# The last batch's Fourier folds queued on VectorE behind the third low part of the first MLP chunk

## The chip, the cores and the metric

The kernel runs on one core of a Trainium2 chip. The metric is the device time of one execution in microseconds (us). The core has a matrix engine, TensorE (PE in the profile), three engines for elementwise work, VectorE (DVE), ScalarE (ACT) and GpSimd (POOL), and SyncE (SP), whose queue issues nearly all DMA transfers here. Each engine works through its own queue in order and waits on semaphores for the others. Operands lie in SBUF, and TensorE's results land in PSUM.

## The reference, cut to what matters

Three blocks follow each other: windowed attention, a block that mixes by a Fourier transform and an MLP, and a gated MLP. The change lies in the second one, and in its overlap with the end of the first:

```python
def _moe_ref(x, w_ch1, w_ch2):              # x: (4, 576, 512)
    X = np.fft.fft(x, axis=1)
    X = np.fft.fft(X, axis=2)
    u = x + np.real(X)
    mu = np.mean(u, axis=-1, keepdims=True)
    var = np.mean((u - mu) ** 2, axis=-1, keepdims=True)
    un = (u - mu) / np.sqrt(var + 1e-06)
    ch = np.maximum(un @ w_ch1, 0.0) @ w_ch2
    return u + ch
```

The weights come as 64-bit floats, and the products are made in three passes with operands split in a high and a low part, so that they are nearly those of float32.

## The kernel before

The residual stream lies in SBUF as `uT`, channels on partitions, 4 batches of 576 tokens side by side. The MLP runs over six chunks of 384 tokens. A chunk begins as soon as its tokens are normalized, so the Fourier transforms of the later batches, the layer norms of the later chunks and the decoding of later weights run beside the MLP of the first chunks. Five kinds of work meet in the stretch that the change touches, from about 136 to 170 us.

**The MLP** (`mlp`, line 683). For each block f of 128 hidden channels, 12 matmuls (`mm3`, lines 130 to 132) make `h` in one of two PSUM buffers; ScalarE takes the relu into the high part `rh` (L717), and VectorE makes the low part `rl` from `h` and `rh` (L718). Three blocks later, at most, 12 matmuls add the second layer into four banks `acc`, and after the last block of a phase VectorE adds them to `uT` (L703). The third `h` needs the first one's buffer back, and so the first `rl`.

**The Fourier transform** (`dft`, line 501). The input is first folded in E, O and F. For the last batch the fold is made in one go, inside the first step of `dft(3)`, by five VectorE instructions: E and O (L464, L465), the sums with the reversed half (L469, L470), and a copy of one column (L473), with two small ones on GpSimd (L471, L474). Then `fold_split` makes high parts on ScalarE (`eh` L482, `oh` L484, `grow` L488) and low parts on GpSimd (`el` L483, `ol` L485, `grow` L489). TensorE reads them later as `g<-tab,eh` and so on; L536 to L538 are the copies and splits between the transform's two stages.

**The layer norm** (`ln`, line 624 on) transposes a chunk into PSUM (L637), copies it to SBUF (L639 on ScalarE), normalizes (L650), transposes it back (L656), copies (L659) and splits it in `xhm` (L661, ScalarE) and `xlm` (L662, GpSimd).

**The decode** (`raw` and `halves`, lines 157 to 172) turns 64-bit weights into a high and a low part, 256 columns at a time: a load `dec_s` on SP's queue (L162), `dec_g` on ScalarE (L165), two VectorE steps (L166, L167), the high part on ScalarE (L171) and the low part on VectorE (L172). It has four staging buffers and four `dec_w`.

**The banks** `g`. The transposes and the transform's matmuls share two PSUM buffers (`gps`, `bufs=2`), given out in turn.

The order within each engine's queue isn't written out. The kernel gives priorities (`soon` raises the layer norms, the transforms and the decode of `rest`, and a relu has one of its own), and a scheduler with a model of durations lays the instructions out when the program is built. `tc.issue_after(i)` adds one constraint to that: what is traced inside it, on i's engine, is placed behind i.

Of the kernel before, what the change touches and what calls it, by code (L numbers as in the profile page):

```python
# [42 lines left out]
RATE = 1.0  # L43
NV = 0
VL = 2
LAG, XPT = (1, 2, 3), 0
PACE = 1.0
FP = ()
# [65 lines left out]
class Kernel:  # L114
# [188 lines left out]
    def load_attn(self, n):  # L303
        if n < B * NB:
# [5 lines left out]
            if j % 3 == 0:  # L310
                self.load_k(b, j // 3)
        if VL <= n < B * NB + VL:
            b, j = divmod(n - VL, NB)
            if j % 2 == 0:
# [352 lines left out]
    def open_mlp(self):  # L667
        self.bp, self.mlp_es = self.pool("mlp", side="right")
        self.low = self.nc.vector
        self.bps, self.bps_es = self.pool("mlp_ps", side="right", space=PSUM)  # L670
        self.rs_ = [(self.bp.tile([128, 384], F32R, name=f"rh{i}"), self.bp.tile([128, 384], F32R, name=f"rl{i}")) for i in range(3)]
        self.nr = self.nq = 0

    def rpair(self, n):
        self.nr += 1
        return self.rs_[self.nr % n]
# [6 lines left out]
    def mlp(self, before, last):  # L683
        nc = self.nc
        V, A = nc.vector, nc.scalar
        pend = []
        st = {}

        def second(g, n, f, rh, rl):
            t = self.sets[f % 8]  # L690
            start, size = CHUNKS[n]
            first, last = f == PHASES[g][0][0], f == PHASES[g][0][-1]
            if first:
                st["acc"] = [self.bps.tile([128, 512], F32, tag=f"acc{c}", name="acc") for c in range(4)]
            acc = st["acc"]
            for c in range(4):
                s = slice(128 * c, 128 * c + 128)
                self.mm3(acc[c][:, 0:size], [(t[:, 2, s], t[:, 3, s], rh, rl)], first=first, last=last)
            if last:
                with self.tc.high_priority(URGENT):  # L700
                    for c in range(4):
                        x = self.uT[:, c, start:start + size]
                        v = V.tensor_tensor(out=x, in0=acc[c][:, 0:size], in1=x, op=ALU.add)  # L703
                self.marks = [v.ins]

        for g, (fs, ns) in enumerate(PHASES):
            for n in ns:
                before(g, n)
                xh, xl, size = self.xh[n], self.xl[n], CHUNKS[n][1]
                for f in fs:  # L710
                    t = self.sets[f % 8]
                    ps = self.bps.tile([128, 512], F32, tag="h", bufs=2, name="h")
                    o = ps[:, 0:size]
                    self.mm3(o, [(t[:, 0, 128 * k:128 * k + 128], t[:, 1, 128 * k:128 * k + 128], xh[:, k], xl[:, k]) for k in range(4)])
                    rh, rl = self.rpair(3)
                    with self.tc.high_priority(URGENT):
                        a = A.activation(out=rh, in_=o, func=AF.Relu)  # L717
                        v = V.scalar_tensor_tensor(out=rl, in0=o, scalar=0.0, in1=rh, op0=ALU.max, op1=ALU.subtract)  # L718
                        self.marks = [a.ins, v.ins]
                    pend.append((g, n, f, rh, rl))  # L720
                    yield 5 * size
                    if len(pend) > 2:
                        second(*pend.pop(0))
                        yield 5 * size
        while pend:
            second(*pend.pop(0))
            if last is not None:
                last()
                last = None
            yield 1500  # L730
# [522 lines left out]
def emit(tc, aps):  # L1253
    with ExitStack() as ctx:
        k = Kernel(ctx, tc, aps)
# [44 lines left out]
        def soon(gen):  # L1300
            while True:
                with tc.high_priority(SOON):
                    w = next(gen, None)
                if w is None:
                    return
                yield w * RATE

        def weave(*gens):
            gens = list(gens)
            while gens:  # L1310
                for g in list(gens):
                    w = next(g, None)
                    if w is None:
                        gens.remove(g)
                    else:
                        yield w / 2

        def norms(*ns):
            for n in ns:
                yield from norm(n)  # L1320

        def norm(n):
            for u in UNITS_OF[n]:
                yield from soon(k.ln(u))
            done.add(n)

        def rest():
            yield from soon(k.decode_f(3))
            done.add(0)
            yield from weave(norms(1, 2), soon(k.dft(2)))  # L1330
            yield from soon(k.dft(3))
            k.dft_es.close()
            p, es = k.pool("late", side="left")
            ctx.enter_context(es)
            k.open_tail(p)
            for i in (6, 7, 8):
                k.open_set(i, p)
            for n in TAIL:
                yield from norm(n)
# [13 lines left out]
        def behind(gen):  # L1353
            marks = None
            while True:
                marks = marks or k.marks
                with ExitStack() as st:
                    for i in marks:
                        st.enter_context(tc.issue_after(i))
                    w = next(gen, None)  # L1360
                if w is None:
                    return
                yield w

        def u_forms(gap):
            yield from spaced(k.decode_u(0), gap)
            gen = k.decode_u(1)
            for _ in range(2):
                next(gen)
                yield gap  # L1370
            while not st7:
                yield None
            for _ in gen:
                yield gap
            for kc in range(2):
                yield from spaced(k.decode_in(kc), gap)
# [16 lines left out]
        def raws2():  # L1393
            for e in range(2):
                k.raws(2, e)
                yield 1000

        rest_ = rest()
        lanes = [[rest_], [decodes((4, 5), D45)], []]

# [7 lines left out]
        def before(g, n):  # L1408
            while n not in done:
                next(rest_)  # L1410
            if n == PHASES[g][1][0]:
                drain(lanes[1])
                if g == 1:
                    lanes[2].append(when(behind(blocks1()), lambda: 3 in done))
                elif g == 2:
                    lanes[1].append(behind(pair(6, G6)))
                    lanes[2].append(behind(blocks()))
                elif g == 3:
                    drain(lanes[0], lanes[2])
                    lanes[1].append(pair(8, G8))  # L1420
                    lanes[2].append(raws2())
# [114 lines left out]
```

## Time and profile before

| | us |
|---|---|
| median of 3 runs | 767.67 (766.78 to 767.84) |
| the profiled execution | 767.85 |
| its span | 766.1 |
| TensorE busy | 746.9 (97%) |
| VectorE busy | 526.7 (69%) |
| ScalarE busy | 352.3 (46%) |
| GpSimd busy | 192.5 (25%) |
| TensorE's granted clock, mean | 0.999 of full speed |

The profile is of one execution. The span runs from its first to its last instruction, and 1.75 us lie around it. The table's busy times overlap. An engine's timeline has one row for an instruction or for a run of equal ones: when it starts, how long it takes, and in brackets how long the engine had been idle and what ended that. An instruction's time in it includes what it waits for after its start.

### The profile page before, as it was taken

To read this page: it belongs to the slowest core of one execution; us is meant where nothing else is said; L and a number is where in the kernel's file an instruction comes from. 1 tells how busy PE (TensorE), PEld (TensorE's weight loads), DVE (VectorE), ACT (ScalarE), POOL (GpSimd) and SP (SyncE) were. 2 spreads that over 40 slices of the span, in tenths; PEclk is the share of its full clock that TensorE was granted. 3 is DMA by queue.
4 is the path that set the end of the run, shared out by engine and by line. 5 is a ranking of instruction groups with operands and counts; after the bars stand their busy time and mean duration, and the time that the engine had idled before them with its cause. 6 is when DMAs were issued, how large, how long until landed. Compare 5 with 4: busy or idle time off the path is not lost.

```text
span 766.1 us, 13950 instructions
## 1 busy us (share of the span) xinstructions
PE 746.9 (97%) x4994; PEld 719.3 (94%) x4994; DVE 526.7 (69%) x1482; ACT 352.3 (46%) x839; POOL 192.5 (25%) x246
## 2 busy tenths in 40 slices
PE   7899799899999999999999999999999999999998
PEld 6788698899999999999999999999999898999897
DVE  4768866983445599884688657646987679674662
ACT  5797986745235556341245324124646454231210
POOL 2354453534213450064421112021102111010100
PEclk9999999999999999999999999999999999999999
DMA  9997761443015888585837923753110141114023
GB/s 263 309 303 237 223 212 45 123 125 124 1 30 179 282 275 295 185 318 172 308 133 297 352 93 136 293 217 124 51 62 24 48 132 32 63 32 134 11 73 123
DMA packets 84773, 123.37 MB, mean 161 GB/s; under 512 B 24416, under 2 KB 61664, under 8 KB 84704
## 3 DMA queue, kind: packets, MB, share of 16 engines
q1 hardware_dynamic: 82912, 119.13, 46.6%
q0 software_dynamic: 576, 2.97, 1.1%
q8 instruction: 39, 0.64, 0.4%
q10 hardware_dynamic: 1216, 0.39, 0.2%
q14 instruction: 30, 0.25, 0.1%
HBM read 91.79 MB, written 30.67 MB: 160 GB/s over the span
## 4 chain that ended last, share of the span: by engine, by line
PE 89%; DVE 5%; DMA 2%; ACT 2%; issue 1%; SPq 0%; POOL 0%; ACTq 0%; DVEq 0%; POOLq 0%
PE w L130 7%; PE w L132 7%; PE w L131 7%; PE g L130 7%; PE g L132 6%; PE g L131 6%; PE c L132 6%; PE c L130 6%; PE c L131 6%; PE acc L132 3%; PE acc L131 3%; PE h L130 3%; PE h L131 3%; PE h L132 3%; PE acc L130 3%; PE sc L328 3%
## 5 line engine op out<-in xcount | busy, mean ns | idle before, releaser
L171 ACT ACTIVATE set<-dec_w 128x256 fp32r<-128x256 f32 x111 | 45.0, 414 | 68.6 <-PE w L131 31.0
L846 POOL TENSOR_TENSOR u<-u 128x384 f32<-128x384 f32 x15 | 18.6, 1243 | 185.0 <-ACT u L845 126.4
L619 POOL TENSOR_TENSOR rq<-rq,mhalf 128x1 f32<-128x1 f32 (+1 forms) x24 | 15.9, 664 | 150.1 <-DVE rq L618 149.0
L335 ACT ACTIVATE s<-s,mx 128x128 f32<-128x128 f32 x144 | 47.6, 392 | 8.3 <-DVE mx L333 8.1
L172 DVE TENSOR_TENSOR set<-dec_w,set 128x256 fp32r<-128x256 f32 x99 | 44.1, 453 | 9.8 <-ACT set L171 3.6
L165 ACT ACTIVATE dec_g<-dec_s 128x256 f32<-128x256 f32 x88 | 37.4, 428 | 26.5 <-DMA dec_s<-in_wi 10.8
L131 PE MATMUL acc<-rl,set 128*128 128x384 f32 x144 | 48.7, 338 | 0.0
L132 PE MATMUL acc<-rh,set 128*128 128x384 f32 x144 | 48.6, 337 | 0.0
L333 DVE CUSTOM_DVE_ANT_0 s<-sc,mask 128x128 f32<-128x128 f32 x144 | 33.2, 284 | 21.6 <-PE sc L328 14.1
L130 PE MATMUL acc<-rh,set 128*128 128x384 f32 x144 | 46.2, 337 | 0.0
L328 PE MATMUL sc<-k,q 128*128 128x128 f32 x288 | 40.5, 284 | 4.9 <-DVE mx L333 2.4
L167 DVE SCALAR_TENSOR_TENSOR dec_w<-dec_g,dec_w 128x256 int32<-128x256 int32 x88 | 42.0, 480 | 3.6 <-ACT dec_g L165 3.3
L846 DVE TENSOR_TENSOR u<-w,u 128x384 f32<-128x384 f32 x44 | 24.3, 552 | 27.1 <-POOL u L846 22.6
L328 PEld LDWEIGHTS sc<-k,q 128*128 128x128 f32 x288 | 36.1, 195 | 6.9 <-issue 3.1
L893 DVE TENSOR_TENSOR uT<-g,uT 128x384 f32<-128x384 f32 x36 | 19.3, 552 | 28.2 <-PE g L132 28.1
L718 DVE SCALAR_TENSOR_TENSOR rl<-h,rh 128x384 fp32r<-128x384 f32 x36 | 19.8, 550 | 23.8 <-ACT rh L717 23.7
L130 PE MATMUL c<-set,set 128*128 128x320 f32 (+2 forms) x120 | 36.2, 303 | 0.0
L132 PE MATMUL c<-set,set 128*128 128x320 f32 (+2 forms) x120 | 36.0, 303 | 0.0
L131 PE MATMUL c<-set,set 128*128 128x320 f32 (+2 forms) x117 | 35.1, 302 | 0.0
L166 DVE TENSOR_SCALAR dec_w<-dec_s 128x256 int32<-128x256 int32 x88 | 31.2, 362 | 4.5 <-DMA dec_s<-in_wo 2.9
L355 PEld LDWEIGHTS pv<-v,pts 128*64 128x64 f32 x576 | 23.5, 137 | 7.8 <-issue 4.2
L845 ACT ACTIVATE u<-w 128x384 f32<-128x384 f32 x29 | 14.1, 486 | 36.0 <-PE w L132 35.1
(383 smaller groups left out, 2604.4 us busy)
## 6 DMA issues: line engine op xcount, KB each, us to landing
dec_s<-in_w SPq DMA_DIRECT2D x64, 256.0 KB, 3.5
v<-in_v SPq DMA_DIRECT2D x16, 520.0 KB, 5.8
xht<-xb SPq DMA_DIRECT2D x10, 768.0 KB, 8.9
xhm<-xb SPq DMA_DIRECT2D x10, 768.0 KB, 7.2
xlm<-xb SPq DMA_DIRECT2D x8, 768.0 KB, 7.9
k<-in_k SPq DMA_DIRECT2D x11, 512.0 KB, 6.5
xf<-u SPq DMA_DIRECT2D x18, 256.0 KB, 2.9
p<-xf SPq DMA_DIRECT2D x24, 192.0 KB, 3.4
```

The lines of the kernel that those rows point to most:

```text
L130: mm(out, lhsT=lh, rhs=rh, start=first and i == 0, stop=False)
L131: mm(out, lhsT=lh, rhs=rl, start=False, stop=False)
L132: mm(out, lhsT=ll, rhs=rh, start=False, stop=last and i == n - 1)
L165: nc.scalar.activation(out=g, in_=s[:, :, 1].bitcast(F32), func=AF.Prelu, scale=2.0 ** -112, alpha=-2.0 ** 32)
L166: nc.vector.tensor_scalar(out=w, in0=s[:, :, 0], scalar1=29, scalar2=None, op0=ALU.logical_shift_right)
L167: nc.vector.scalar_tensor_tensor(out=w, in0=g[:].bitcast(I32), scalar=3, in1=w, op0=ALU.logical_shift_left, op1=ALU.bitwise_or)
L171: self.nc.scalar.activation(out=hi, in_=f, func=AF.Copy)
L172: self.low.tensor_tensor(out=lo, in0=f, in1=hi, op=ALU.subtract)
L328: nc.tensor.matmul(sc[:, hp], lhsT=q[:, hp].rearrange("p a b -> p (a b)"), rhs=k[:, hp, o:o + 128], start=True, stop=True)
L333: nc.vector.tensor_tensor_reduce(out=s[:, hp], in0=sc[:, hp], in1=mask, scale=-0.125, scalar=1e30, op0=ALU.add, op1=ALU.min, accum_out=mx[ ...
L335: nc.scalar.activation(out=s[:, hp], in_=s[:, hp], func=AF.Exp, bias=mx[:, hp:hp + 1], scale=-1.0)
L846: add = lambda eng, o, i, j: eng.tensor_tensor(out=o, in0=i, in1=j, op=ALU.add)
```

## The change

The MLP keeps a list of its low-part instructions. The first step of the last batch's transform, which holds its fold, is traced inside `issue_after` of the third of them (`BEHIND = 2`, counted from 0), so the fold's VectorE instructions must stand behind it. The rest of the transform is traced as before. No instruction is added or removed; the scheduler lays out the stretch around the fold anew, on all engines.

```diff
+BEHIND = 2
...
         self.nr = self.nq = 0
+        self.lows = []
...
                         v = V.scalar_tensor_tensor(out=rl, in0=o, scalar=0.0, in1=rh, op0=ALU.max, op1=ALU.subtract)
                         self.marks = [a.ins, v.ins]
+                    self.lows.append(v.ins)
...
-            yield from soon(k.dft(3))
+            yield from soon(held(k.dft(3)))
...
+        def held(gen):
+            with tc.issue_after(k.lows[BEHIND]):
+                w = next(gen)
+            yield w
+            yield from gen
```

Line numbers of the changed kernel are 1 higher than before from line 46 on, 2 from line 674 on and 3 from line 720 on, so L464 is L465 there, and L718 is L720.

On VectorE, from the fold to the first low part, the order before is this (`rl_2201` belongs to the first block's `h`; `set_...` are weights):

```order
L464 TENSOR_TENSOR E<-uT 128x1152
L465 TENSOR_TENSOR O<-uT 128x1152
L166 TENSOR_SCALAR dec_w<-dec_s 128x256 x2
L469 TENSOR_TENSOR E<-E 128x2x288
L166 TENSOR_SCALAR dec_w<-dec_s 128x256 x2
L470 TENSOR_TENSOR F<-O 128x2x288
L473 COPY F<-O 128x2
L167 SCALAR_TENSOR_TENSOR dec_w<-dec_g,dec_w 128x256 x2
L718 SCALAR_TENSOR_TENSOR rl_2201<-h,rh_2200 128x384
```

After the change VectorE has the fold between the third low part (`rl_2199`) and the fourth (again `rl_2201`, the first one's buffer):

```order
L720 SCALAR_TENSOR_TENSOR rl_2199<-h,rh_2198 128x384
L465 TENSOR_TENSOR E<-uT 128x1152
L466 TENSOR_TENSOR O<-uT 128x1152
L167 TENSOR_SCALAR dec_w<-dec_s 128x256
L173 TENSOR_TENSOR set_2190<-dec_w,set_2190 128x256
L168 SCALAR_TENSOR_TENSOR dec_w<-dec_g,dec_w 128x256
L173 TENSOR_TENSOR set_2190<-dec_w,set_2190 128x256
L470 TENSOR_TENSOR E<-E 128x2x288
L471 TENSOR_TENSOR F<-O 128x2x288
L474 COPY F<-O 128x2
L720 SCALAR_TENSOR_TENSOR rl_2201<-h,rh_2200 128x384
L168 SCALAR_TENSOR_TENSOR dec_w<-dec_g,dec_w 128x256
```

Ahead of the first low part there now stand four L166 and two L167 of the decode alone.

On ScalarE, at the end of the decode's run beside the first chunk, the order before has the layer norm's first copy of the next chunk, L639, ahead of the last two `set` copies:

```order
L171 ACTIVATE set_2191<-dec_w 128x256
L165 ACTIVATE dec_g<-dec_s 128x256
L537 ACTIVATE tail0b<-cp 33x256
L171 ACTIVATE set_2191<-dec_w 128x256
L165 ACTIVATE dec_g<-dec_s 128x256
L639 ACTIVATE u<-g 128x512
L171 ACTIVATE set_2191<-dec_w 128x256 x2
L717 ACTIVATE rh_2202<-h 128x384
```

After the change it stands behind them, and the split of the fold comes just before:

```order
L483 ACTIVATE eh<-E 128x2x289
L489 ACTIVATE grow<-gr 1x289
L662 ACTIVATE xhm<-u 128x4x128
L537 ACTIVATE cp<-g 33x256
L485 ACTIVATE oh<-F 128x2x289
L172 ACTIVATE set_2191<-dec_w 128x256
L166 ACTIVATE dec_g<-dec_s 128x256
L538 ACTIVATE tail0b<-cp 33x256
L172 ACTIVATE set_2191<-dec_w 128x256 x2
L640 ACTIVATE u<-g 128x512 x2
L719 ACTIVATE rh_2202<-h 128x384
```

Both copies of the layer norm now follow each other directly, behind every `set` copy.

## Rows read from the trace of the kernel before

**Rows 1.** The page, chain that ended last, its share by engine.

```profile
PE 89%; DVE 5%; DMA 2%; ACT 2%; issue 1%; SPq 0%; POOL 0%; ACTq 0%; DVEq 0%; POOLq 0%
```

**Rows 2.** TensorE's waits, 134 to 210 us: us in total, times, longest.

```profile
PE h L130 <- DVE rl L718: 1.5, 1, 1.5
...
PE g L656 <- DVE uT L568: 0.2, 1, 0.2
```

**Rows 3.** Timeline of TensorE: start, us, engine, line, operation, tiles, count, [idle before].

```profile
141.88 0.86 PE L130 MATMUL acc<-rh,set 128*128 128x384 f32 x4
...
145.35 0.44 PE L130 MATMUL h<-xh,set 128*128 128x384 f32 x1 [1.46 <-DVE rl L718]
...
149.62 0.33 PE L130 MATMUL h<-xh,set 128*128 128x384 f32 x1
149.79 0.34 PE L131 MATMUL h<-xl,set 128*128 128x384 f32 x1
...
160.10 0.60 PE L637 MATMUL g<-ident,uT 128*128 128x128 f32 x4
```

**Rows 4.** Timeline of VectorE, the fold and the first low part.

```profile
136.94 1.36 DVE L464 TENSOR_TENSOR E<-uT 128x1152 f32<-128x1152 f32 x1 [0.55 <-ACT uT L386]
138.22 1.35 DVE L465 TENSOR_TENSOR O<-uT 128x1152 f32<-128x1152 f32 x1
...
140.52 0.75 DVE L469 TENSOR_TENSOR E<-E 128x576 f32<-128x576 f32 x1
...
142.21 0.75 DVE L470 TENSOR_TENSOR F<-O 128x576 f32<-128x576 f32 x1
142.88 1.29 DVE L473 COPY F<-O 128x2 f32<-128x2 f32 x1
...
144.75 0.54 DVE L718 SCALAR_TENSOR_TENSOR rl<-h,rh 128x384 fp32r<-128x384 f32 x1
```

**Rows 5.** Timeline of VectorE, third and fourth low part, decode steps between.

```profile
152.09 0.54 DVE L718 SCALAR_TENSOR_TENSOR rl<-h,rh 128x384 fp32r<-128x384 f32 x1
152.55 0.41 DVE L172 TENSOR_TENSOR set<-dec_w,set 128x256 fp32r<-128x256 f32 x1
...
154.64 0.41 DVE L167 SCALAR_TENSOR_TENSOR dec_w<-dec_g,dec_w 128x256 int32<-128x256 int32 x1
154.97 0.28 DVE L166 TENSOR_SCALAR dec_w<-dec_s 128x256 int32<-128x256 int32 x1
155.78 0.91 DVE L172 TENSOR_TENSOR set<-dec_w,set 128x256 fp32r<-128x256 f32 x1 [0.53 <-ACT set L171]
156.61 1.54 DVE L167 SCALAR_TENSOR_TENSOR dec_w<-dec_g,dec_w 128x256 int32<-128x256 int32 x1
...
158.82 0.54 DVE L718 SCALAR_TENSOR_TENSOR rl<-h,rh 128x384 fp32r<-128x384 f32 x1
```

**Rows 6.** Timeline of GpSimd, low parts of fold, layer norm and transform.

```profile
141.19 0.95 POOL L489 TENSOR_TENSOR grow<-gr,grow 1x289 fp32r<-1x289 f32 x1 [0.56 <-ACT grow L488]
142.22 1.93 POOL L483 TENSOR_TENSOR el<-E,eh 128x578 fp32r<-128x578 f32 x1
...
154.68 1.73 POOL L662 TENSOR_TENSOR xlm<-u,xhm 128x512 fp32r<-128x512 f32 x1 [2.66 <-ACT xhm L661]
156.37 1.50 POOL L485 TENSOR_TENSOR ol<-F,oh 128x578 fp32r<-128x578 f32 x1
157.94 0.81 POOL L538 TENSOR_TENSOR tail0b<-cp,tail0b 33x256 fp32r<-33x256 f32 x1
```

**Rows 7.** Timeline of ScalarE, first decode steps and the layer norm's copy.

```profile
138.93 0.75 ACT L165 ACTIVATE dec_g<-dec_s 128x256 f32<-128x256 f32 x2
...
158.82 0.59 ACT L639 ACTIVATE u<-g 128x512 f32<-128x512 f32 x1
```

**Rows 8.** The staged weights `dec_s`, 125 to 175 us: time from issue to landing.

```profile
DMA to landing us min/median/max: 2.6/3.4/4.9
```

**Rows 9.** The tile `eh`, 170 to 215 us: count, ns min/median/max, first and last start.

```profile
L130 PE MATMUL g<-tab,eh x6: 279/288/386, 183.5 to 186.0; 128*128 128x258 f32 x4, 128*33 128x258 f32 x2
```

## The prediction

> **What bounds the kernel now.** I read the page's chain first: TensorE (PE) holds 89% of it [rows 1], so a saved or added microsecond counts where it ends or makes a wait of TensorE. The list of TensorE's waits in the stretch in which the change lies comes next: the longest is 1.5 us, a first-layer matmul that waits for the low part `rl` of a relu [rows 2]. The timeline shows the place: the third `h` group starts at 145.35 after 1.46 us of idleness [rows 3]. There are two `h` buffers in PSUM, so the third group needs the first group's low part, and that stands on VectorE (DVE) behind the folds. VectorE's timeline shows them: E and O at 136.94 and 138.22, the reversed pair at 140.52 and 142.21, a copy of two elements that takes 1.29 us, and only at 144.75 the low part [rows 4]. The reader should see there that the folds are not the whole delay: decode steps stand between them, and several VectorE instructions are longer than their shape asks for. GpSimd (POOL) explains those. The copy ends at 144.17, and POOL's `el` ends at 144.15 [rows 4, 6]; a decode step of 0.41 us takes 1.54 us from 156.61 to 158.15 while POOL's `ol` runs to 157.87 [rows 5, 6]. So the two engines take turns, and POOL's work is a term of any sum for VectorE.
>
> **What the change removes.** The folds' five VectorE instructions leave the place ahead of the first low part. Behind them now stand four first decode steps (L166) whose data lie in SBUF, two L167, and then `rl`. ScalarE (ACT) gives the two `dec_g` at 138.93 to 139.68 [rows 7] and the first relu right after, some half a microsecond, so the first low part comes at about 140.1 in place of 144.75, and TensorE, which has work until 143.89 (145.35 less 1.46), no longer waits. Removed: 1.46 us.
>
> **What it adds.** The folds now stand behind the third low part and ahead of the fourth, and the scheduler has moved decode, layer-norm copies and fold splits with them. Which wait ends last then? The candidate is the second group of transposes L637. It needs a `g` bank, which ScalarE's first copy L639 gives back. In the order before, that copy stood ahead of the last decode copies L171; now it stands behind all of them, and each L171 needs an L167 of VectorE. Before, L639 ran at 158.82 and the transposes at 160.10 without a wait [rows 3, 7]. I add up when L639 can run now.
>
> Steps by themselves: L167 or L172 take 0.34 us from start to start, L166 0.21 (0.28 less the overlap of 0.07), a low part 0.47 [rows 5]; E and O together 2.55, L469 and L470 0.67 each (0.75 less 0.08 of overlap), the copy some 0.1 without POOL [rows 4]. POOL by itself, its wait for VectorE taken off: `ol` 1.18 (from 156.69, where L172 ends, to 157.87); `el` 1.19 (L470 ends at 142.96, `el` at 144.15); `bl` or tail 0.60 (158.15 to 158.75); `grow` 0.67 (0.95 less 0.28); `xlm` 1.16 (from 155.25, where L166 ends, to 156.41) [rows 4 to 6]. I call them 1.2, 1.2, 0.6, 0.7 and 1.2. For `gr`, which works on one partition like `grow`, I take 0.7, and 0.2, an estimate, for its one-element copy.
>
> First, the start. VectorE has read the staged weights early, so the next load waits only for ScalarE's first `dec_g`, done at about 139.35, and for the queue: 139.4. Landing takes 2.6 to 4.9 us, median 3.4 [rows 8]; I take 3.0, since the queue is empty then: 142.4. From there to the third low part stand five L166 (1.05), eight L167 or L172 (2.7), two low parts (0.94) and POOL's `xlm` and `bl` (1.8): 6.5, so 148.9. Then E and O 2.55, four decode steps 1.2, POOL's `xlm`, `bl`, `gr` and its copy 2.7, the reversed pair and copy 1.45, the fourth low part 0.47: 8.4, so 157.3. Behind it eight decode steps (three L166, five L167 or L172) 2.3, against POOL's `el`, `grow`, `xlm`, `ol` and tail, 4.9: 164.5. ScalarE's last L171 (0.3) and L639 (0.59 [rows 7]) put the transposes at 165.4.
>
> What would cost nothing? In the new order 76 and not 69 matmuls of 384 columns stand between the four `acc` matmuls at 141.88 and these transposes, counted in the two orders; the seven take 0.17 each (149.62 to 149.79), 1.2 us [rows 3]. So the transposes may come at 160.10 + 1.2 = 161.3 with no net change, and at 159.85 for the whole gain of 1.46. The sum says 165.4: a loss of 4.1.
>
> How good is such a sum? I make the same one for the order before. From E at 136.94 to the first low part: own work 5.5 and POOL 2.8 give 145.2, and the trace has 144.75 [rows 4]. From the third low part, 152.09, to the fourth: 0.47, twelve decode steps 3.56 and POOL's three instructions 3.0 give 159.1, and the trace has 158.82 [rows 5]. The sums are 0.45 us too long in 7.8 and 0.3 in 6.7, about 5%. Over the 23 us from 142.4 that is 1.15: the transposes come at 164.25, a loss of 2.95. I take **+2.9 us**. It includes the 1.46 removed. It should last to the end, since TensorE is the chain and its order behind the hunk is unchanged.
>
> Other edits. The same number of instructions runs on each engine. The last batch's transform reads `eh` first at 183.5 [rows 9], and in the sum `eh` is ready near 157 and `ol` near 163: more than 20 us hide the folds' delay, and without that cover all of it, some 15 us, would show. The queue SP has the same loads in a slightly other order; a later landing is in the bounds below.
>
> **A rule beside the rows.** Two VectorE instructions at 154.64 and 154.97 take 0.41 and 0.28 us undisturbed though POOL's `xlm` had begun at 154.68 [rows 5, 6]: POOL does not get its turn after each instruction. The Trainium skill, page "SBUF — State Buffer", section "SBUF: two separate sides", calls the pair of ports that VectorE and GpSimd share an exclusive lock, held for a whole instruction by whichever starts first. By that rule strictly taken the turns alternate and the uncorrected sum, +4.1, holds; the row at 154.97 speaks for less.
>
> **The rivals.** *VectorE keeps its pace, and no new wait comes.* What costs is POOL's work between VectorE's steps, 1.8 + 2.7 + 4.9 = 9.4 us in the sum. If a third of it, 2.95, falls into VectorE's idle time (it waits for loads and for ScalarE) the transposes come by 161.3 and the change is level; with half, 4.4, by 159.85, and only the 1.46 gain stands: 767.85 - 1.46 = 766.4, by the median 766.2. For it speaks the row at 154.97; against it the 1.54 and 0.91 us steps right behind [rows 5]. Not slower: 26% for level, and 6% for more than that, where the small wait of 0.2 us behind a VectorE step of the transform [rows 2] goes as well: 1.66 us, 766.0.
>
> *The loads land late.* With the longest landing, 4.9 us [rows 8], the first step is 1.9 later, and all behind it: +4.8, 772.5. The crowded stretch speaks for it, the empty queue at 139.4 against it: 10%.
>
> **How the numbers follow.** The profiled execution took 767.85 us, its span 766.1 and 1.75 around it; 767.85 + 2.9 = 770.75. It lies 0.18 above the median of the runs, so I predict 770.6 us: 58%. Late loads add 10% on the same side, so slower by over 0.2% (1.5 us, about what a measurement can tell from no change) has 68%, within 0.2% 26%, faster 6%. The forecast's own range is 769.2 (half of the loss) to 771.8 (the sum uncorrected). The range of all cases runs from 766.6, near the whole gain, which leaves about a tenth below, to 772.4, just short of the latest loads.
>
> **What would show it.** Right: the first low part at about 140, no wait of the third `h` group; the fourth low part at 156 to 158; POOL busy almost without a break from there for 5 us, and decode steps of over 1 us beside it; the second L637 transposes near 164 with the longest wait of the stretch, put down to ScalarE's L639. Wrong: these transposes at or before 161, or a first `h` wait that remains. If an `h` or `acc` matmul waits for the fourth low part instead, the mechanism is the folds themselves and not the copy behind the decode.

## The result and the profile after

The changed kernel takes 771.1 us (median of 12 runs, 769.15 to 775.47) against 767.75 us (12 runs, 766.33 to 770.89) of the kernel before, run beside it: a ratio of 1.0051, 95% interval 1.0038 to 1.0064. It is slower, by 3.4 us by the medians' difference; 770.6 us had been forecast. The profiled execution took 770.25 us, its span 768.4 us, so 1.85 us lie around it.

Two profiled executions also differ where nothing was changed, so I compare all kernels here between two fixed points: the start of the four `acc` matmuls in one row, which was at 141.88 before [rows 3], and the start of the `tail0b` matmul of the second half of a later transform, at 197.89 before. That is 56.01 us before, and 59.07 after (141.66 to 200.73): **+3.06 us**. The granted clock is 1.00 between the two points in both. Ahead of the first point the changed kernel's execution was 0.22 us shorter and behind the second about half a microsecond, which leaves the 2.4 us between the two profiled times.

TensorE's waits after, 134 to 210 us (us in total, times, longest), which answer [rows 2]:

```profile
PE g L638 <- ACT u L640: 2.4, 1, 2.4
PE h L131 <- ACT xhm L662: 1.0, 1, 1.0
PE xt L385 <- DVE rq L621: 0.8, 1, 0.8
PE h L132 <- POOL xlm L663: 0.5, 1, 0.5
PE g L657 <- DVE uT L569: 0.2, 1, 0.2
```

The wait of the third `h` group for the low part is gone; `xt` and L657 wait as before. Three waits are new, and TensorE's timeline, in the columns of [rows 3], shows where:

```profile
156.29 0.34 PE L132 MATMUL acc<-rl,set 128*128 128x384 f32 x1
157.67 0.63 PE L131 MATMUL h<-xhm,set 128*128 128x384 f32 x2 [1.03 <-ACT xhm L662]
...
159.55 0.34 PE L133 MATMUL acc<-rh,set 128*128 128x384 f32 x1
160.38 0.45 PE L132 MATMUL h<-xlm,set 128*128 128x384 f32 x1 [0.50 <-POOL xlm L663]
...
161.37 0.34 PE L131 MATMUL h<-xhm,set 128*128 128x384 f32 x1
164.12 0.66 PE L638 MATMUL g<-ident,uT 128*128 128x128 f32 x4 [2.42 <-ACT u L640]
```

They sum to 3.95 us, less the 1.46 removed 2.49. Between the two fixed points TensorE's busy time rises as well, from 54.31 to 54.88 us with the same work, and 2.49 + 0.57 is the whole 3.06. Most of the 0.57 belongs to the waits too. A row's time is 0.33 to 0.34 us though the next matmul of this shape starts after 0.17 [rows 3], so the idle time in brackets begins some 0.17 us after TensorE has begun to stand still. From start to start, less the usual step, the three waits cost 1.21, 0.66 and 2.58 us. The one before cost 1.62, counted from this row of the trace before to the third `h` group at 145.35:

```profile
143.61 0.28 PE L132 MATMUL g<-tab,ol 128*128 128x256 f32 x1
```

The first rows behind a wait also take 0.06 to 0.11 us longer to the next one (0.28 for 0.17 at 160.38, 0.41 for 0.35 at 164.12). Counted in this way the new waits make 4.73 us and the old one 1.73, and the difference, 3.00, is all but 0.06 of the 3.06.

VectorE's timeline after, from the third low part on (it answers [rows 4, 5]):

```profile
148.18 0.54 DVE L720 SCALAR_TENSOR_TENSOR rl<-h,rh 128x384 fp32r<-128x384 f32 x1
148.64 1.34 DVE L465 TENSOR_TENSOR E<-uT 128x1152 f32<-128x1152 f32 x1
149.91 1.34 DVE L466 TENSOR_TENSOR O<-uT 128x1152 f32<-128x1152 f32 x1
151.18 0.28 DVE L167 TENSOR_SCALAR dec_w<-dec_s 128x256 int32<-128x256 int32 x1
...
153.06 0.75 DVE L471 TENSOR_TENSOR F<-O 128x576 f32<-128x576 f32 x1
153.72 1.26 DVE L474 COPY F<-O 128x2 f32<-128x2 f32 x1
154.90 0.54 DVE L720 SCALAR_TENSOR_TENSOR rl<-h,rh 128x384 fp32r<-128x384 f32 x1
155.37 0.48 DVE L168 SCALAR_TENSOR_TENSOR dec_w<-dec_g,dec_w 128x256 int32<-128x256 int32 x1
155.77 2.48 DVE L167 TENSOR_SCALAR dec_w<-dec_s 128x256 int32<-128x256 int32 x2
158.16 1.03 DVE L173 TENSOR_TENSOR set<-dec_w,set 128x256 fp32r<-128x256 f32 x1
159.12 1.49 DVE L168 SCALAR_TENSOR_TENSOR dec_w<-dec_g,dec_w 128x256 int32<-128x256 int32 x1
160.54 1.40 DVE L167 TENSOR_SCALAR dec_w<-dec_s 128x256 int32<-128x256 int32 x1
...
162.20 0.94 DVE L168 SCALAR_TENSOR_TENSOR dec_w<-dec_g,dec_w 128x256 int32<-128x256 int32 x1
```

Behind the fourth low part at 154.90 most of the decode steps that take 0.28 and 0.41 us elsewhere take 0.9 to 1.5 us. GpSimd's timeline shows its side (as [rows 6]):

```profile
150.14 4.82 POOL L663 TENSOR_TENSOR xlm<-u,xhm 128x512 fp32r<-128x512 f32 x1 [3.38 <-ACT xhm L662]
154.92 0.64 POOL L539 TENSOR_TENSOR bl<-cp,bh 128x256 fp32r<-128x256 f32 x1
155.53 0.97 POOL L472 TENSOR_TENSOR gr<-O 1x288 f32<-1x288 f32 x1
156.45 0.17 POOL L475 COPY gr<-O 1x1 f32<-1x1 f32 x1
156.58 1.31 POOL L484 TENSOR_TENSOR el<-E,eh 128x578 fp32r<-128x578 f32 x1
157.97 0.95 POOL L490 TENSOR_TENSOR grow<-gr,grow 1x289 fp32r<-1x289 f32 x1
158.99 1.34 POOL L663 TENSOR_TENSOR xlm<-u,xhm 128x512 fp32r<-128x512 f32 x1
160.29 1.50 POOL L486 TENSOR_TENSOR ol<-F,oh 128x578 fp32r<-128x578 f32 x1
161.87 0.98 POOL L539 TENSOR_TENSOR tail0b<-cp,tail0b 33x256 fp32r<-33x256 f32 x1
```

From 154.92 to 162.85 it is busy almost without a break. And ScalarE's timeline (as [rows 7]) joins the two to TensorE:

```profile
156.65 0.45 ACT L489 ACTIVATE grow<-gr 1x289 fp32r<-1x289 f32 x1 [2.62 <-POOL gr L475]
157.00 0.61 ACT L662 ACTIVATE xhm<-u 128x512 fp32r<-128x512 f32 x1
...
160.65 0.42 ACT L172 ACTIVATE set<-dec_w 128x256 fp32r<-128x256 f32 x1 [1.24 <-DVE dec_w L168]
...
163.17 0.42 ACT L172 ACTIVATE set<-dec_w 128x256 fp32r<-128x256 f32 x1 [2.10 <-DVE dec_w L168]
163.49 0.58 ACT L640 ACTIVATE u<-g 128x512 f32<-128x512 f32 x1
```

The last row is the copy that gives the `g` bank back. It ran at 158.82 before [rows 7] and runs now at 163.49, right behind the last decode copy, which waited 2.10 us for VectorE; TensorE's transposes come out of it at 164.12. The first two rows are the other new wait: `xhm` stands behind the fold's `grow`, and `grow` waits for GpSimd's `gr`, which stood behind the 4.82 us `xlm`.

### The profile page after: what moved, and what is told of

Read it like the earlier page. It is cut to its first block, busy times and chain, and to the rows that moved or that the text cites. A ratio compares the mean times of both kernels' runs of the same rounds, so it can differ in the third digit from the quotient of the medians.

```text
span 768.4 us, 13956 instructions
## 1 busy us (share of the span) xinstructions
PE 747.6 (97%) x4994; PEld 719.8 (94%) x4994; DVE 529.0 (69%) x1482; ACT 352.5 (46%) x839; POOL 194.9 (25%) x246
## 4 chain that ended last, share of the span: by engine, by line
PE 76%; DVE 2%; issue 1%; ACT 0%; POOL 0%
PE w L131 7%; PE w L133 7%; PE w L132 7%; PE c L133 6%; PE c L131 6%; PE c L132 6%; PE g L131 6%; PE g L133 6%; PE g L132 6%; PE h L133 3%; PE h L132 3%; PE acc L131 3%; PE h L131 3%; PE acc L133 3%; PE acc L132 3%; PE g L638 1%
## 5 line engine op out<-in xcount | busy, mean ns | idle before, releaser
L620 POOL TENSOR_TENSOR rq<-rq,mhalf 128x1 f32<-128x1 f32 (+1 forms) x24 | 16.0, 665 | 148.9 <-DVE rq L619 147.8
L173 DVE TENSOR_TENSOR set<-dec_w,set 128x256 fp32r<-128x256 f32 x99 | 45.0, 463 | 9.3 <-PE h L132 3.3
L166 ACT ACTIVATE dec_g<-dec_s 128x256 f32<-128x256 f32 x88 | 37.4, 429 | 24.7 <-DMA dec_s<-in_wi 10.0
L334 DVE CUSTOM_DVE_ANT_0 s<-sc,mask 128x128 f32<-128x128 f32 x144 | 33.3, 284 | 21.6 <-PE sc L329 14.5
L720 DVE SCALAR_TENSOR_TENSOR rl<-h,rh 128x384 fp32r<-128x384 f32 x36 | 19.9, 552 | 23.5 <-ACT rh L719 23.5
L167 DVE TENSOR_SCALAR dec_w<-dec_s 128x256 int32<-128x256 int32 x88 | 31.5, 368 | 5.2 <-DMA dec_s<-in_wo 2.0
```

The costliest lines, as they stand in the source:

```text
L166: nc.scalar.activation(out=g, in_=s[:, :, 1].bitcast(F32), func=AF.Prelu, scale=2.0 ** -112, alpha=-2.0 ** 32)
L167: nc.vector.tensor_scalar(out=w, in0=s[:, :, 0], scalar1=29, scalar2=None, op0=ALU.logical_shift_right)
L173: self.low.tensor_tensor(out=lo, in0=f, in1=hi, op=ALU.subtract)
L334: nc.vector.tensor_tensor_reduce(out=s[:, hp], in0=sc[:, hp], in1=mask, scale=-0.125, scalar=1e30, op0=ALU.add, op1=ALU.min, accum_out=mx[ ...
```

## The experiments

My theory after the result: the loss is made on one chain, GpSimd's low parts between VectorE's decode steps, then the decode copies on ScalarE, then the layer norm's copy behind them, then the transposes. The rivals take the fold itself, or the loss of one place in a queue, for the cause. Ratios below are to the kernel before on the same chip, 767.24 us (35 runs) beside the first four and 767.02 us (29 runs) beside the last three; "between the fixed points" is as above, from one profiled execution of each, and the granted clock in that stretch is 1.00 in all of them. Line numbers are each kernel's own.

| fold behind low part | between the fixed points, us | against before | ratio (interval) |
|---|---|---|---|
| none asked (before) | 56.01 | | |
| first | 58.22 | +2.21 | 1.0028 (1.0016 to 1.0040) |
| third (the change) | 59.07 | +3.06 | 1.0051 (1.0038 to 1.0064) |
| third, copy ahead of the decode | 58.07 | +2.06 | 1.0026 (1.0012 to 1.0039) |
| third, no `el`, `ol` | 56.80 | +0.79 | 1.0006 (0.9996 to 1.0017) |
| third, both edits | 56.39 | +0.38 | 0.9997 (0.9985 to 1.0009) |
| fourth | 54.92 | -1.09 | 0.9982 (0.9970 to 0.9994) |
| fifth | 54.42 | -1.59 | 0.9980 (0.9967 to 0.9993) |
| sixth | 54.62 | -1.39 | 0.9989 (0.9976 to 1.0003) |

**The layer norm's copy ahead of the last decode copies.**

```diff
-        self.nc.scalar.activation(out=hi, in_=f, func=AF.Copy)
+        self.his.append(self.nc.scalar.activation(out=hi, in_=f, func=AF.Copy).ins)
...
-            A.activation(out=u[:r], in_=ps[:r], func=AF.Copy)
+            c = A.activation(out=u[:r], in_=ps[:r], func=AF.Copy)
+            if n == 2 and i == 0:
+                for h in self.his[-2:]:
+                    self.tc.add_manual_dep(h, c.ins.name, ...)
```

> The changed kernel with one edge more: on ScalarE the last two decode copies stand behind the layer norm's first copy of the next chunk, as before the change. Theory one (VectorE and GpSimd, sharing, are late with the decode, and the copy is only the first to show it): the copy ends near 160, the second transposes no longer wait (2.4 us gone), but VectorE's additions into uT still follow the decode at 164, so the next wait, of the second layer's banks, takes about half back: 1.0 to 1.5 us less than the changed kernel, still slower than before by 1.5 to 2.5. Rival (the copy's place alone is the loss): the whole 2.4 us come back and the time is within 0.5 us of before or a little under it.

Measured: 768.36 us, about half of the loss back by the ratios (1.0026 for 1.0051), a third (1.00 us) between the fixed points. The copy runs at 157.99 and the transposes come at 160.06 without a wait. TensorE's waits and timeline show what takes its place:

```profile
PE h L131 <- ACT xhm L665: 1.0, 1, 1.0
PE h L131 <- DVE rl L723: 0.8, 1, 0.8
PE xt L385 <- DVE rq L621: 0.8, 1, 0.8
PE h L132 <- POOL xlm L666: 0.5, 1, 0.5
```

```profile
164.51 1.22 PE L131 MATMUL acc<-rh,set 128*128 128x384 f32 x4
166.54 0.45 PE L131 MATMUL h<-xhm,set 128*128 128x384 f32 x1 [0.81 <-DVE rl L723]
```

The 2.4 us are gone, and an `h` group now waits 0.8 us for a low part that stands on VectorE behind the same slow decode and the additions into `uT` that follow it. Theory one had looked for the next wait at the second layer's banks; there the four `acc` matmuls only take 1.22 us for the 0.86 of others. From start to start the two together cost 1.3 us: 2.03 from 164.51 to 166.54, for 0.69 before (148.93 to 149.62). The order isn't the changed kernel's in one more thing: two of the additions into `uT` now stand ahead of the last two L173. So the copy behind the decode is a cause, and not the whole one; the rival, by which its place was the whole loss, falls.

**No low parts of the last fold.** The kernel leaves out a part of the computation.

```diff
+            old = dict(zip(("eh", "el", "oh", "ol"), self.fp.get(b - 1, ())))
-            self.fp[b] = [self.dp.tile(...) for n in ("eh", "el", "oh", "ol")]
+            self.fp[b] = [old[n] if b == B - 1 and n[1] == "l" else self.dp.tile(...) for n in ("eh", "el", "oh", "ol")]
...
-        G.tensor_tensor(out=el, in0=E[:, :, a:z], in1=eh, op=ALU.subtract)
+        if b < B - 1:
+            G.tensor_tensor(out=el, in0=E[:, :, a:z], in1=eh, op=ALU.subtract)
...
-        G.tensor_tensor(out=ol, in0=F[:, :, a:z], in1=oh, op=ALU.subtract)
+        if b < B - 1:
+            G.tensor_tensor(out=ol, in0=F[:, :, a:z], in1=oh, op=ALU.subtract)
```

> The changed kernel without GpSimd's two low parts of the last batch's fold, el and ol (the last batch's transform reads those of the batch before it, so a part of the computation is left out). The order on VectorE and ScalarE around the fold stays. Theory one (GpSimd's instructions make VectorE's decode steps wait): el and ol took 1.3 and 1.5 us between the decode steps, so the layer norm's copy comes 2.2 to 2.8 us earlier, at about 161, and the transposes wait for 0 to 0.4 us instead of 2.4: 2 to 3 us less than the changed kernel. Rival (the fold's own 4 us on VectorE and the order are the loss, GpSimd is beside it): the copy stays at 163.5 and the time that of the changed kernel, within 0.5 us.

Measured: 767.33 us, the ratio within 0.2% of 1, and 2.27 us less than the changed kernel between the fixed points. ScalarE's timeline at its end:

```profile
161.24 0.42 ACT L172 ACTIVATE set<-dec_w 128x256 fp32r<-128x256 f32 x1 [0.97 <-DVE dec_w L168]
161.56 0.58 ACT L643 ACTIVATE u<-g 128x512 f32<-128x512 f32 x1
```

The copy still stands behind the decode, but comes at 161.56, and the transposes at 162.20 wait 0.27 us. VectorE's folds are all there, in the same order: two GpSimd instructions of 1.2 us each between VectorE's steps cost 2.3. What is left, 2.4 us over the fold behind the fifth low part, isn't divided between the folds, the order and GpSimd's other work. Nor is the +0.79 a comparison of like with like: the kernel before was not run without `el` and `ol`, and there `el` runs beside the copy of 1.29 us ahead of the first low part [rows 4, 6].

**The fold behind the first low part, and behind the fifth.** `BEHIND = 0` and `BEHIND = 4`.

```diff
-BEHIND = 2
+BEHIND = 0
```

> The fold behind the first low part (BEHIND = 0): the first low part is freed, all else of the fold stays as early as it can. Theory one (what hurts is the fold and GpSimd's work on it in the midst of the decode, whatever the place): the 1.46 us wait goes, and waits of in all 2.5 to 3.5 us come for low parts and for the layer norm's copy: 1 to 2 us over before. Rival (only the place behind the third hurts, since the copies are reordered there): 1 to 1.5 us under before.

> The fold behind the fifth low part (BEHIND = 4) in place of the third. The decode of the stretch is then over when the fold comes. Theory one: no wait of the third h group, no wait of the second transposes: 1.2 to 1.8 us under before, 766.0 to 766.5. Rival (a fold that is queued behind relus at all delays the last transform or the next layer norm): no better than before, since the fold is first read at 183.5 and stands now at 164 or later; a new wait of TensorE near 180 to 186.

Measured: 769.15 and 765.32 us. Behind the first, TensorE's waits are these:

```profile
PE acc L132 <- DVE rl L720: 1.0, 2, 0.5
PE g L638 <- ACT u L640: 1.0, 1, 1.0
```

The loss is a little over the 1 to 2 us that I expected. The transposes wait here too, 0.97 us at 162.84, but less, since part of the GpSimd work is done early (`el` at 147.29), and `acc` matmuls wait for low parts behind the fold. Behind the fifth all these waits are gone, and what is left are two of TensorE's waits, of which only the second grew against before, from 0.2 us [rows 2]; it lies at 180.24, where the rival had looked for a new one:

```profile
PE xt L385 <- DVE rq L621: 0.8, 1, 0.8
PE g L657 <- DVE uT L569: 0.6, 1, 0.6
```

The transposes come at 158.12 without a wait. It is faster than both kernels, by 0.2% than the one before.

**Behind the fourth and the sixth.** `BEHIND = 3` and `BEHIND = 5`, the two places next to the fifth.

> The folds stand behind the fourth low part in place of the third, one place ahead of the version behind the fifth, which gained 1.6 us between two fixed points. In the order ScalarE's layer-norm copy of the second group of transposes now stands ahead of the fold's split `eh`, but behind `grow`, which waits for GpSimd's `gr`, which waits for VectorE's O. Theory one (a place is good or bad by what then stands in a row ahead of that copy): a wait of about 0.7 to 1.3 us of these transposes remains, and a small one of an `acc` matmul on the next low part; 0.5 to 1.2 us slower than before: 768.2 to 768.9, and the decode is no longer what the copy waits for. Rival (the decode alone makes the loss, and here the last decode copies stand ahead of E): no wait is left, the gain of 1.46 stands: about 766.

> The folds stand behind the sixth low part, one place behind the version that gained. Theory one (what counts is that neither the low parts nor the layer norm's copies wait for the folds, and the transform reads their parts only near 183): the same gain again, 765.0 to 766.3, no wait of an `h`, `acc` or transposes row over 0.3 us. Rival (each place further back brings the folds' work nearer to the transform's own VectorE and GpSimd steps, which wait grows): a wait for `uT` or for `eh`, `ol` of over 1 us, 766.5 to 768.

Measured: 765.81 and 765.70 us. The sixth does what theory one says, with no wait over 0.3 us but that of `xt`; the interval of its ratio, though, just reaches 1.0003. For the fourth theory one's numbers fell: I had expected 0.5 to 1.2 us over the kernel before, and it is 1.09 under it, near the rival's 766. The chain that I named is there, in ScalarE's timeline and in TensorE's:

```profile
158.31 0.45 ACT L489 ACTIVATE grow<-gr 1x289 fp32r<-1x289 f32 x1 [4.96 <-POOL gr L475]
158.66 0.57 ACT L640 ACTIVATE u<-g 128x512 f32<-128x512 f32 x1
```

```profile
159.29 0.66 PE L638 MATMUL g<-ident,uT 128*128 128x128 f32 x4 [0.36 <-ACT u L640]
```

The copy does stand behind `grow`, but its delay reaches TensorE with 0.36 us and not 0.7 to 1.3, and no `acc` matmul waits. What differs from the third place is the decode: its last copies are on ScalarE at 150.73, ahead of all of this. Between the third and the fourth place lies a step of 4.15 us between the fixed points, and in the order of VectorE it is the last run of decode steps that now stands ahead of E, all but two L173. The rest of the order differs between the two places as well, so that the decode makes the step is argued from the traces and not shown by itself.

**Both edits together**, on the change as it is.

> The two cuts together: the last two decode copies stand behind the layer norm's copy, and GpSimd's low parts `el` and `ol` of the last batch are left out (the transform reads those of the batch before, so this part of the computation is missing). Each alone took back 2 to 3 us of the changed kernel's loss. Theory one (both shorten one and the same chain, GpSimd between VectorE's decode steps, decode copies, layer norm's copy, transposes): they don't add. The transposes already came within 0.3 us of no wait with the low parts left out, so 0.0 to 0.5 us less than that version: 766.8 to 767.4; the waits on `xhm` (1.0) and `xlm` (0.5), which stand ahead of both cuts, remain, and no wait on `rl`. Rival (two separate losses): the gains add, 765.0 or less.

Measured: 766.74 us, just under theory one's 766.8 and far from the rival's 765.0. Between the fixed points it is 0.41 us less than without the low parts alone: the gains of 1.00 and 2.27 us make 2.68 and not 3.27, so more than half of the smaller one lies in the other, as on one chain. (The "2 to 3 us" for each in the expectation are 1.00 and 2.27 by this measure.) What remains of its waits stands ahead of both cuts:

```profile
PE h L131 <- ACT xhm L668: 1.1, 1, 1.1
```

`xlm` waits 0.18 us more. These two make 1.27 us, less than the 1.46 removed, and the stretch is still 0.38 longer than before, again with TensorE's busy time above that of before (54.87 us for 54.31). From start to start, with the slower first rows, the two waits cost 1.81 us and the removed one 1.73, which explains 0.08 of the 0.38; the other 0.3 lies in no single wait and stays without a cause.

## Why the prediction was right

**The bound and the removed wait.** Right: the first low part starts at 139.88 (forecast: about 140.1, and this execution runs 0.22 us ahead there), and no `h` group waits for it.

**The new wait.** Right in kind, place and cause: the second group of transposes at 164.12 (forecast 164.25), with the longest wait of the stretch, put down to ScalarE's layer-norm copy. The first experiment took this copy out of its place and its wait went; the second left it there and took the GpSimd work away, and most of the loss went (2.27 of 3.06 us).

**The sum.** Right at its end, but not inside. To the end of the third low part it gave 148.9; the trace has 148.64, where E starts. For the fold with the fourth low part it gave 8.4 us, to 157.3; the trace has 6.73, to 155.37, where the next decode step starts. For the decode behind it 7.2 us; the trace has 7.77, to 163.14. The step that failed is where GpSimd's instructions fall. I had put `xlm`, `bl`, `gr` and its copy between VectorE's fold steps; of these only `xlm` got in, after 3.7 us of waiting (4.82 less 1.16), and the others moved behind the fourth low part. So the fourth low part came at 154.90 and not at 156 to 158. Both sides of that line lead to the same copy, so the errors of -1.7 and +0.6 leave 14.5 us where the sum had 15.6, about the 5% (here 7%) by which I had cut the sum. But the moved work did not cost its full time: with GpSimd's 1.5 us moved, the sum's own figures give 8.7 us behind the line, and the trace has 7.77, so about 1 us of the two engines' work overlapped there. Some 0.45 us of it is `bl`, which starts at 154.92 beside the fourth low part and does not hold it up (0.54 us). That the cut of 1.15 us came out right is in part luck; where the overlap would lie was not foreseen.

**The size.** +3.06 us between the fixed points, +2.9 forecast. By the forecast TensorE would stand still 4.4 us in one wait (164.25 less 159.85); it does for 4.45 from start to start, in three (3.95 by the idle time in brackets). The waits on `xhm` and `xlm`, 1.53 us together, were not foreseen: I had followed ScalarE's order behind the copy L639 and not ahead of `xhm`, where `grow` now waits for GpSimd. They cost little more, because the later wait for the copy is shorter by what TensorE idled before it; the combined experiment shows what they are worth alone, when the chain behind them is short. The slower first rows behind each wait, 0.28 us after the change for 0.11 before, were not in the sum either.

**The fold's readers.** Right: `eh` is first read at 186.4, and `ol` is done at 161.79, 24 us earlier. Behind the fifth `ol` ends at 169.21 and `oh` is first read at 183.69, still without a wait.

**The rule beside the rows.** By strict turns, as the rule of the Trainium skill, page "SBUF — State Buffer", section "SBUF: two separate sides" (an exclusive lock: of a GpSimd instruction and a VectorE instruction in a 2-port mode or with two SBUF inputs, whichever starts first has the shared pair for the whole instruction), was read there, the loss was to be 4.1 us. The trace comes near to strict turns behind 155 us (7.77 us for the 8.7 of both engines' own work) and not before: `xlm` waited through several VectorE instructions.

**The rivals.** The level outcome needed a third of GpSimd's work in VectorE's idle time; from 154.92 to 162.85 VectorE has no idle time at all, and most of its steps are two to five times as long. Of the 9.4 us only about 1 was hidden, by overlap. Late loads were not seen: the first decode step behind them starts at 142.66 (142.4 in the sum), and the time to the third low part was met within 0.3 us.

**What the prediction left out.** It said that the fold's delay is hidden by 20 us, and stopped there. That same cover allows a later place, and one low part further back the sign turns.

## What to carry to other kernels

An instruction that is moved takes its whole group with it, and the scheduler fills the old place with other work: ask for each engine which copy or eviction now stands behind the moved group, and who waits for its bank. The price of elementwise work on VectorE depends on what GpSimd has queued at that time; count both engines' own times in one sum, and trust the sum's end more than where in it each piece falls. When a place is good or bad by what stands in a row with it, try the neighbouring places too: here the third was 0.5% slower and the fourth and fifth 0.2% faster than the order before.

## What the runs showed of the hardware

GpSimd can be held off for long by VectorE. The `xlm` at 150.14 takes 4.82 us for some 1.2 us of work, while VectorE runs seven instructions at full pace (O to F); it takes 4.83 and 4.82 us in the first two experiments. Taking its 1.16 us off its end gives 153.80, and VectorE's F ends at 153.81. Before the change `el` got in at the same copy, where L470 ends at 142.96 [rows 4, 6]. (GpSimd's spans are the roughest of the profile; I rely on ends that agree.) In the version behind the fourth low part VectorE's and GpSimd's timelines show another way in:

```profile
150.62 0.41 DVE L168 SCALAR_TENSOR_TENSOR dec_w<-dec_g,dec_w 128x256 int32<-128x256 int32 x1
151.63 0.70 DVE L167 TENSOR_SCALAR dec_w<-dec_s 128x256 int32<-128x256 int32 x1 [0.61 <-DMA dec_s<-in_w]
```

```profile
148.97 3.22 POOL L663 TENSOR_TENSOR xlm<-u,xhm 128x512 fp32r<-128x512 f32 x1 [3.39 <-ACT xhm L662]
```

Here `xlm` ends at 152.19, and 1.16 us before that is 151.03, just where VectorE's step ends and its wait for a load begins. Behind the fifth and the sixth it is the same: `xlm` takes 3.22 and 3.23 us and ends 1.16 us after the step ahead of the wait. Once in, the two nearly take turns: behind 155.4 after the change most decode steps have a GpSimd instruction beside them, and GpSimd does not wait for several of them again. What lets GpSimd in at the two-element copy at 153.72, with VectorE's queue full, and not between the steps ahead of it, was not tried and stays open.
